# Gathers of an expert's tokens placed behind the last scatter-add of the expert two places ahead, in a mixture-of-experts kernel

## The chip, the cores and the metric

The kernel runs on one core of one Trainium2 chip. Its time is the device time of one execution in microseconds (us), as a median of three runs. Clocks of TensorE are given as the share of full speed that was granted.

## The reference

The program is a chain of three blocks on 2304 tokens of width 512: a linear attention with exponential features, a dense two-layer block with a squared ReLU, and a mixture of 8 experts, each token going to its two best. The change touches the third block alone:

```python
def _moe2_ref(x, w_gate, w_noise, noise, w1, w2):      # x: 2304 x 512, w1: 8 x 512 x 1024, w2: 8 x 1024 x 512
    noisy_logits = x @ w_gate + np.log1p(np.exp(x @ w_noise)) * noise
    top2 = np.argpartition(-noisy_logits, 2, axis=1)[:, :2]
    ...
    for e in range(E):
        for k in range(2):
            mask = top2[:, k] == e
            h = np.maximum(x[mask] @ w1[e], 0.0)
            out[mask] += top2_w[mask, k, None] * (h @ w2[e])
```

## The kernel before

Products are made in 16-bit floating point with every operand split into a high and a low half, so that each product is three matmuls. The dense block leaves its result, rows of 1024 halves, in DRAM (`x2d`). A router writes for each expert a list of 640 slots in five tiles of 128 (`ix`, `ww`: token and weight of each slot).

The experts then go one after the other. For each one the work is:

- **Gather and transpose** (`c_gather`, L583 to L587): GpSimd issues an indirect DMA that fetches the 128 rows of one tile from DRAM into a buffer `g`, of which there are four, and SyncE issues a DMA that transposes it into `xg`. `xg` holds one expert's five tiles and has two buffers: the transposes of expert e+1 need the one that expert e-1 used. Expert 0's first four tiles are gathered earlier, its fifth and all of expert 1's in `c_slots`, during expert 0.
- **First product** (L702): eight tiles of 12 matmuls with 512 columns (`c_main`), then 96 matmuls with 128 columns for the fifth tile of tokens (`c_tail`). The results go to PSUM buffers `c1`, of which there are four. ScalarE (L709) and VectorE (L710) turn each into the halves `hm` of the activation, which frees the buffer.
- **Second product** (L773): five tiles of 24 matmuls. ScalarE scales each result into `y` (L779, three buffers), and GpSimd issues an indirect DMA that adds it to rows of the output (L780). Two scatter-adds can name the same row, so each waits until the one ahead of it has landed.
- **Weights of the next expert** (`c_piece`, L574): eight pieces of 512 KB. For each one ScalarE issues a DMA from DRAM into a staging buffer `stg` (L293, three buffers), makes the high half (L294), and VectorE the low half (L295). These instructions stand in the same queues as L709, L710 and L779, and an engine's queue goes in order: a DMA that ScalarE can't issue yet holds up all that stands behind it.

TensorE's order is the order of the code. For the other engines a scheduler sets the order when the program is built, and it also gives each DMA of SyncE and ScalarE one of eight semaphores (`DMAHW0` to `DMAHW7`, called lanes below), in turn, and each of GpSimd one of `DMASW0` to `DMASW7`. A DMA that gets a lane waits until the lane's last user has landed, unless the program knows that already.

A call of `gathers(e + 1)` stands at the head of expert e (L750 to L751). The scheduler may place its instructions anywhere from there on, or ahead of work that stands earlier in the code, as the buffers allow.

Of the kernel before, what the change touches and what calls it, by code (L numbers as in the profile page):

```python
# [14 lines left out]
ALU = mybir.AluOpType  # L15
# [27 lines left out]
def moe_kernel(tc, qT, kT, v, omT, omD, w_in, w_out, wgn, noise, w1, w2, out):  # L43
    nc = tc.nc
# [523 lines left out]
    def c_weights(e):  # L568
        wp = hC if e % 2 else cP
        a = wp.tile([P, 2, 4, FE], F16, name="w1t", tag="w1t", bufs=1)  # L570
        b = wp.tile([P, 2, 8, DM], F16, name="w2t", tag="w2t", bufs=1)
        W[e] = a, b

    def c_piece(e, j):  # L574
        a, b = W[e]
        if j < 4:
            s = slice(j * 256, (j + 1) * 256)
            split(a[:, 0, :, s], a[:, 1, :, s], w1s[e][:, :, s], [4, 256], SW1)
        else:
            s = slice(j * 2 - 8, j * 2 - 6)  # L580
            split(b[:, 0, s, :], b[:, 1, s, :], w2s[e][:, s, :], [2, 512], SW2)

    def c_gather(xg, t, ix, c, rows=N + P):  # L583
        g = cP.tile([P, 2 * DM], F16, name="g", tag="g", bufs=4)
        nc.gpsimd.indirect_dma_start(out=g, out_offset=None, in_=x2d[0:rows, :],  # L585
                                     in_offset=bass.IndirectOffsetOnAxis(ap=ix[:, c:c + 1], axis=0))
        nc.sync.dma_start_transpose(xg[:, t], g)  # L587
# [3 lines left out]
    def new_xg(e):  # L591
        XG[e] = cP.tile([P, CT, 8, P], F16, name="xg", tag="xg", bufs=2)
# [112 lines left out]
    def c_main(fc, a, xg, e):  # L705
        ps = psC.tile([P, MAIN], F32, name="c1", tag="c1", bufs=4)
        c_mm1(ps, a, e, fc, lambda c: xg[:, 0:4, c, :], lambda c: xg[:, 0:4, 4 + c, :])
        h = hC.tile([P, 2, MAIN], F16, name="hm", tag="hm", bufs=12)
        nc.scalar.activation(h[:, 0], ps, AF.Relu)  # L709
        nc.vector.scalar_tensor_tensor(h[:, 1], ps, 0.0, h[:, 0], ALU.max, ALU.subtract)  # L710
        return h

    def c_tail(g, a, xg, e):
        ps = psC.tile([P, 4, P], F32, name="c1t", tag="c1", bufs=4)
        for i in range(4):
            c_mm1(ps[:, i, :], a, e, 4 * g + i, lambda c: xg[:, 4, c, :], lambda c: xg[:, 4, 4 + c, :])
        h = hC.tile([P, 2, 4, P], F16, name="ht", tag="ht", bufs=3)
        nc.scalar.activation(h[:, 0], ps, AF.Relu)
        nc.vector.scalar_tensor_tensor(h[:, 1], ps, 0.0, h[:, 0], ALU.max, ALU.subtract)
        return h  # L720
# [4 lines left out]
    ix = ww = pm = pg = sp_i = tok = None  # L725

    def c_slots():
        nonlocal ix, ww, pm, pg, sp_i, tok
        next(r5, None)
        ix, ww = slots(0, NCOL, "f")  # L730
        pm = const.tile([P, 1], F32, name="pm")
        nc.vector.tensor_reduce(pm, pall.rearrange("p t k -> p (t k)"), AX.X, ALU.max)
        pg = const.tile([P, 1], F32, name="pg")
        nc.gpsimd.partition_all_reduce(pg, pm, P, bass_isa.ReduceOp.max)
        sp_i = const.tile([P, 1], I32, name="sp_i")
        nc.vector.tensor_copy(sp_i, pg)
        tok = const.tile([P, NT], I32, name="tok")
        nc.gpsimd.iota(tok, [[P, NT]], base=P, channel_multiplier=1)
        c_gather(XG[0], 4, ix, 4)
        gathers(1)  # L740

    def gathers(e):
        new_xg(e)
        for t in range(CT):
            c_gather(XG[e], t, ix, CT * e + t)

    for e in range(NE):
        if e + 1 < NE:
            c_weights(e + 1)
        if 0 < e < NE - 1:  # L750
            gathers(e + 1)  # L751
        a, b = W[e]
        xg = XG[e]
        hm = []
        for fc in range(8):
            hm.append(c_main(fc, a, xg, e))
            if e + 1 < NE:
                c_piece(e + 1, fc)
            if e == 0 and fc in (2, 6):
                next(r5, None)  # L760
        ht = []
        for t in range(CT):
            if t == (3 if e == 0 else 0):
                ht = [c_tail(g, a, xg, e) for g in range(2)]
            ps = psM.tile([P, DM], F32, name="c2", tag="mm", bufs=3)
            n = 0
            for fc in range(8):
                for hl, wl in ((0, 0), (0, 1), (1, 0)):
                    if t < 4:
                        st = hm[fc][:, hl, t * P:(t + 1) * P]  # L770
                    else:
                        st = ht[fc // 4][:, hl, fc % 4, :]
                    nc.tensor.matmul(ps, st, b[:, wl, fc, :], start=n == 0, stop=n == 23)  # L773
                    n += 1
            if e == 0 and t == 0:
                c_slots()
            c = CT * e + t
            y = hC.tile([P, DM], F32, name="y", tag="y", bufs=3)
            nc.scalar.activation(y, ps, AF.Copy, scale=ww[:, c:c + 1])  # L779
            nc.gpsimd.indirect_dma_start(out=out, out_offset=bass.IndirectOffsetOnAxis(ap=ix[:, c:c + 1], axis=0),  # L780
                                         in_=y, in_offset=None, compute_op=ALU.add)
    cctx.close()

    mctx.close()
# [6 lines left out]
    with tc.If(spill > CAP - 1):  # L791
        for e in range(NE):
# [8 lines left out]
            with tc.For_i(0, NT) as t:  # L801
# [19 lines left out]
                for fc in range(8):  # L821
                    for hl, wl in ((0, 0), (0, 1), (1, 0)):
                        nc.tensor.matmul(ps, h[:, hl, fc, :], b[:, wl, fc, :], start=n == 0, stop=n == 23)
                        n += 1
                y = oP.tile([P, DM], F32, name="oy", tag="oy", bufs=1)
                nc.scalar.activation(y, ps, AF.Copy, scale=sc)
                nc.gpsimd.indirect_dma_start(out=out, out_offset=bass.IndirectOffsetOnAxis(ap=oi, axis=0),
                                             in_=y, in_offset=None, compute_op=ALU.add)
# [43 lines left out]
```

## Time and profile before

| | |
|---|---|
| median of three runs | 966.22 us (965.87, 966.22 and 968.92) |
| profiled execution | 967.28 us, of which the span of instructions is 965.4 us |
| mean granted TensorE clock | 0.970 |
| TensorE matmul busy | 914.7 us, 95% of the span |
| VectorE, ScalarE, GpSimd busy | 469.4, 441.7 and 113.0 us |
| mean DMA rate | 131 GB/s |

Times in the profile count from the start of the span. PE is TensorE, DVE VectorE, ACT ScalarE, POOL GpSimd and SP SyncE; a name with q (ACTq, SPq, POOLq) is the engine's queue, which issues DMAs. Idle time of an engine in square brackets names what ended it.

### The profile page before, as it was taken

How to read it: one execution, taken by the hardware profiler on the slowest of the kernel's cores; microseconds unless marked ns; L12 is line 12 of the kernel's file. 1: busy time of each engine (PE TensorE's matmuls, PEld its weight loads, DVE VectorE, ACT ScalarE, POOL GpSimd, SP SyncE). 2: the span in 40 equal slices, each digit the busy share in tenths (PEclk: the TensorE clock that was granted, in tenths of full speed). 3: DMA queues.
4: the chain of work that ended last, by engine and by line, in shares of the span. 5: the costliest groups of instructions: out<-in, count | busy, mean ns of one | idle time of the engine just before them, and what ended most of it. 6: DMA issues, size and time to landing. Idle time of an engine off the chain costs nothing.

```text
span 965.4 us, 15725 instructions
## 1 busy us (share of the span) xinstructions
PE 914.7 (95%) x6254; PEld 501.2 (52%) x6254; DVE 469.4 (49%) x983; ACT 441.7 (46%) x912; POOL 113.0 (12%) x134
## 2 busy tenths in 40 slices
PE   7679799899999999999999997999999999999994
PEld 4546455555655655654654452545454545445451
DVE  4798986772772783584642723333240514230110
ACT  5979975752852862563622423333231423231210
POOL 1000000000000000000001142232222131211111
PEclk8779899999999999999999998999999999999997
DMA  7894787329342114227207499975768595831212
GB/s 240 230 242 136 186 229 170 82 78 296 76 95 66 49 45 99 55 51 183 73 21 171 146 206 212 231 166 117 161 131 175 135 204 121 177 53 24 31 19 40
DMA packets 174723, 126.08 MB, mean 131 GB/s; under 512 B 121744, under 2 KB 147472, under 8 KB 174640
## 3 DMA queue, kind: packets, MB, share of 16 engines
q1 hardware_dynamic: 143072, 74.47, 33.0%
q0 software_dynamic: 9024, 21.08, 12.3%
q10 hardware_dynamic: 22544, 29.43, 10.0%
q8 instruction: 51, 0.84, 0.4%
q14 instruction: 32, 0.26, 0.1%
HBM read 75.15 MB, written 20.45 MB: 99 GB/s over the span
## 4 chain that ended last, share of the span: by engine, by line
PE 71%; ACT 6%; DVE 5%; DMA 5%; issue 2%; POOL 0%; POOLq 0%; DVEq 0%; ACTq 0%
PE s L356 19%; PE c L773 18%; PE c L702 16%; PE s L339 10%; PE c1t L702 4%; ACT ef L175 2%; DMA xg<-g 2%; PE pj L160 2%; DMA out_dram<-y,ix_f 2%; DMA stg<-in_w_dram 1%; DVE r L347 1%; DVE h L348 1%; ACT r L343 1%; ACT eq L179 1%; DVE nm L168 1%
## 5 line engine op out<-in xcount | busy, mean ns | idle before, releaser
L339 PE MATMUL s<-xT,wi 128*128 128x384 f16 x1152 | 198.2, 330 | 3.8 <-ACT r L343 3.7
L356 PE MATMUL s<-wo,h 128*128 128x512 f16 x864 | 192.8, 381 | 3.3 <-ACT r L343 3.3
L702 PE MATMUL c<-xg,w1t 128*128 128x512 f16 x768 | 171.0, 384 | 6.7 <-DVE hm L710 6.6
L702 PEld LDWEIGHTS <-w1t 128*128 128x128 f16 x1536 | 119.2, 98 | 102.0 <-issue 12.1
L773 PE MATMUL c<-w2t,hm 128*128 128x512 f16 x768 | 167.4, 379 | 0.0
L339 PEld LDWEIGHTS <-wi 128*128 128x128 f16 x1152 | 110.8, 99 | 78.6 <-issue 8.2
L356 PEld LDWEIGHTS <-h 128*128 128x128 f16 x864 | 83.5, 98 | 102.1 <-issue 5.7
L773 PEld LDWEIGHTS <-hm 128*128 128x128 f16 x768 | 74.8, 98 | 88.5
L779 ACT ACTIVATE y<-c,ww_f 128x512 f32<-128x512 f32 x40 | 27.5, 687 | 156.1 <-PE c L773 100.8
L295 DVE SCALAR_TENSOR_TENSOR w2t<-stg,w2t 128x1024 f16<-128x1024 f32 x32 | 38.1, 1222 | 124.1 <-ACT w2t L294 124.1
L175 ACT ACTIVATE ef<-pj,nm 128x128 f32<-128x128 f32 x248 | 74.1, 383 | 42.2 <-DVE nm L168 42.1
L780 POOL DMA_INDIRECT out_dram<-y,ix_f x40 | 62.8, 1571 | 170.9 <-ACT y L779 77.2
L710 DVE SCALAR_TENSOR_TENSOR hm<-c,hm 128x512 f16<-128x512 f32 x64 | 43.2, 687 | 78.5 <-ACT hm L709 78.4
L709 ACT ACTIVATE hm<-c 128x512 f16<-128x512 f32 x64 | 37.2, 593 | 66.8 <-PE c L702 60.2
L160 PE MATMUL pj<-om,raw 64*128 64x128 f32 x576 | 51.1, 304 | 13.6 <-ACT ef L175 10.5
L347 DVE TENSOR_TENSOR r<-r 128x384 f32<-128x384 f32 x96 | 53.2, 554 | 16.3 <-ACT r L343 14.4
L343 ACT ACTIVATE r<-s 128x384 f32<-128x384 f32 x96 | 47.3, 494 | 23.2 <-PE s L339 21.3
L348 DVE TENSOR_TENSOR h<-r,h 128x384 f16<-128x384 f32 x96 | 53.4, 556 | 7.6 <-ACT h L345 2.7
L160 PEld LDWEIGHTS pj<-om,raw 64*128 64x128 f32 x576 | 41.7, 202 | 28.5 <-ACT ef L175 12.6
L295 DVE SCALAR_TENSOR_TENSOR w1t<-stg,w1t 128x1024 f16<-128x1024 f32 x32 | 37.8, 1223 | 35.8 <-ACT w1t L294 35.8
L585 POOL DMA_INDIRECT g<-x2d,ix_f x36 | 38.8, 1079 | 135.5 <-DMA xg<-g 127.6
L168 DVE TENSOR_REDUCE nm<-pj 128x4 f32<-128x512 f32 x72 | 47.6, 683 | 9.6 <-PE pj L160 9.6
(158 smaller groups left out, 873.6 us busy)
## 6 DMA issues: line engine op xcount, KB each, us to landing
stg<-in_w_dram ACTq DMA_DIRECT2D x56, 512.0 KB
stg<-in_w_in_dram SPq DMA_DIRECT2D x16, 512.0 KB
stg<-in_w_out_dram SPq DMA_DIRECT2D x16, 512.0 KB
out_dram<-zero SPq DMA_DIRECT2D x19, 256.0 KB
raw<-in_kT_dram SPq DMA_DIRECT2D x9, 512.0 KB
vr<-in_v_dram SPq DMA_DIRECT2D x18, 256.0 KB
raw<-in_qT_dram SPq DMA_DIRECT2D x9, 512.0 KB
x2d<-x SPq DMA_DIRECT2D x18, 256.0 KB
```

Of the source, the lines that this page charges most:

```text
L160: nc.tensor.matmul(pj[g][:, j, :], raw[s, j, :], om[s, :], start=True, stop=True)
L168: nc.vector.tensor_reduce(nm, pj, AX.X, ALU.max, negate=True)
L175: nc.scalar.activation(ef[:, i, :], pj[:, i, :], AF.Exp, bias=nm[:, i:i + 1])
L295: nc.vector.scalar_tensor_tensor(dst_l, stg, scale, dst_h, ALU.mult, ALU.subtract)
L339: nc.tensor.matmul(ps, wi[:, wl, c, fc * P:(fc + 1) * P], x[:, :, xl + c, :], start=n == 0, stop=n == 11)
L343: nc.scalar.activation(r, ps, AF.Relu, scale=SH / (SX * SWI))
L347: nc.vector.tensor_tensor(r2, r, r, ALU.mult)
L348: nc.vector.tensor_tensor(h[:, 1], r2, h[:, 0], ALU.subtract)
L356: nc.tensor.matmul(ps, hs[fc][:, hl, j * P:(j + 1) * P], wo[:, wl, fc, :], start=fc == 0 and k == 0, stop=fc == 15 and k == 2)
L702: nc.tensor.matmul(ps, a[:, wl, c, fc * P:(fc + 1) * P], mv(c), start=n == 0, stop=n == 11)
L773: nc.tensor.matmul(ps, st, b[:, wl, fc, :], start=n == 0, stop=n == 23)
L780: nc.gpsimd.indirect_dma_start(out=out, out_offset=bass.IndirectOffsetOnAxis(ap=ix[:, c:c + 1], axis=0), in_=y, in_offset=None, compute_op ...
```

## The change

The gathers of experts 2 to 7 are told to be issued behind an instruction: the last scatter-add of the expert two places ahead of them. `tc.issue_after` adds no wait on a semaphore, it only fixes the order in GpSimd's queue. Two lines of code move by one or two, so L780 of before is L781 after.

```diff
--- before.py
+++ after.py
@@ -748,7 +748,8 @@
         if e + 1 < NE:
             c_weights(e + 1)
         if 0 < e < NE - 1:
-            gathers(e + 1)
+            with tc.issue_after(added.ins):
+                gathers(e + 1)
         a, b = W[e]
         xg = XG[e]
         hm = []
@@ -777,8 +778,9 @@
             c = CT * e + t
             y = hC.tile([P, DM], F32, name="y", tag="y", bufs=3)
             nc.scalar.activation(y, ps, AF.Copy, scale=ww[:, c:c + 1])
-            nc.gpsimd.indirect_dma_start(out=out, out_offset=bass.IndirectOffsetOnAxis(ap=ix[:, c:c + 1], axis=0),
-                                         in_=y, in_offset=None, compute_op=ALU.add)
+            added = nc.gpsimd.indirect_dma_start(out=out,
+                                                 out_offset=bass.IndirectOffsetOnAxis(ap=ix[:, c:c + 1], axis=0),
+                                                 in_=y, in_offset=None, compute_op=ALU.add)
     cctx.close()
```

GpSimd's queue before, from the second scatter-add of expert 0 to the gathers behind expert 1's scatter-adds (`g` is a gather, `out_dram` a scatter-add; the three gathers at the head are expert 1's last and expert 2's first two):

```order
L780 DMA out_dram<-y,ix_f 2432x512
L585 DMA g<-x2d,ix_f 128x1024 x3
L780 DMA out_dram<-y,ix_f 2432x512
L585 DMA g<-x2d,ix_f 128x1024 x6
L780 DMA out_dram<-y,ix_f 2432x512
L585 DMA g<-x2d,ix_f 128x1024
L780 DMA out_dram<-y,ix_f 2432x512
L585 DMA g<-x2d,ix_f 128x1024 x4
L780 DMA out_dram<-y,ix_f 2432x512
L585 DMA g<-x2d,ix_f 128x1024
L780 DMA out_dram<-y,ix_f 2432x512 x4
L585 DMA g<-x2d,ix_f 128x1024 x4
```

The same queue after, from the same scatter-add on; the one gather ahead of the three scatter-adds is expert 1's last:

```order
L781 DMA out_dram<-y,ix_f 2432x512
L585 DMA g<-x2d,ix_f 128x1024
L781 DMA out_dram<-y,ix_f 2432x512 x3
L585 DMA g<-x2d,ix_f 128x1024 x5
L781 DMA out_dram<-y,ix_f 2432x512 x5
L585 DMA g<-x2d,ix_f 128x1024 x5
L781 DMA out_dram<-y,ix_f 2432x512 x5
```

Before, gathers of up to two experts ahead stand among an expert's scatter-adds; after, five scatter-adds of one expert and five gathers of the expert two places behind it take turns, to the end.

SyncE's transposes keep their order but get other lanes. Before, from the transpose of expert 0's last tile on (then expert 1's five, then expert 2's first three); the last `DMAHW` that a row names is the lane that it takes (one ahead of it guards the buffer), and where none is named its lane was known to be free:

```order
L587 DMA_TRANSPOSE xg<-g 128x8x128 [waits DMAHW0_49,DMASW6_49]
L587 DMA_TRANSPOSE xg<-g 128x8x128 [waits DMAHW1_49,DMASW7_49]
L587 DMA_TRANSPOSE xg<-g 128x8x128 [waits DMAHW2_49,DMASW0_49]
L587 DMA_TRANSPOSE xg<-g 128x8x128 [waits DMAHW3_49,DMASW1_49]
L587 DMA_TRANSPOSE xg<-g 128x8x128 [waits DMAHW4_49,DMASW3_49]
L587 DMA_TRANSPOSE xg<-g 128x8x128 [waits DMAHW5_49,DMASW5_49]
L587 DMA_TRANSPOSE xg<-g 128x8x128 [waits DMAHW0_49,DMAHW6_49,DMASW6_49,PE_49]
L587 DMA_TRANSPOSE xg<-g 128x8x128 [waits DMAHW7_49,DMASW7_49]
L587 DMA_TRANSPOSE xg<-g 128x8x128 [waits DMASW1_49]
```

The first six rows are the same after; the seventh, expert 2's first tile, takes lane 6 before and lane 3 after. ScalarE's queue before, at the end of expert 0 and the start of expert 1 (the loads of `stg` are pieces of expert 2's weights):

```order
L293 DMA stg<-in_w_dram 128x4x256 [waits DMAHW2_49,DVE_49]
L293 DMA stg<-in_w_dram 128x2x512 [waits DMAHW3_49,DVE_49]
L779 ACTIVATE y<-c_6872,ww_f 128x512 [waits DMASW2_49,PE_49]
L294 ACTIVATE w1t<-stg 128x4x256 [waits DMAHW2_49]
L293 DMA stg<-in_w_dram 128x2x512 [waits DMAHW5_49,DVE_49]
L293 DMA stg<-in_w_dram 128x2x512 [waits DMAHW6_49,DVE_49]
L779 ACTIVATE y<-c_6900,ww_f 128x512 [waits DMASW4_49,PE_49]
L294 ACTIVATE w2t<-stg 128x1024 [waits DMAHW3_49]
L294 ACTIVATE w2t<-stg 128x1024 [waits DMAHW5_49]
L709 ACTIVATE hm<-c_6946 128x512 [waits PE_49]
L294 ACTIVATE w2t<-stg 128x1024 [waits DMAHW6_49]
L293 DMA stg<-in_w_dram 128x2x512 [waits DMAHW7_49,DVE_49]
```

The same twelve rows after:

```order
L293 DMA stg<-in_w_dram 128x4x256 [waits DVE_49]
L293 DMA stg<-in_w_dram 128x2x512 [waits DVE_49]
L780 ACTIVATE y<-c_6872,ww_f 128x512 [waits DMASW2_49,PE_49]
L294 ACTIVATE w1t<-stg 128x4x256 [waits DMAHW6_49]
L293 DMA stg<-in_w_dram 128x2x512 [waits DMAHW0_49,DVE_49]
L293 DMA stg<-in_w_dram 128x2x512 [waits DMAHW1_49,DVE_49]
L780 ACTIVATE y<-c_6900,ww_f 128x512 [waits DMASW4_49,PE_49]
L294 ACTIVATE w2t<-stg 128x1024 [waits DMAHW7_49]
L294 ACTIVATE w2t<-stg 128x1024 [waits DMAHW0_49]
L709 ACTIVATE hm<-c_6946 128x512 [waits PE_49]
L294 ACTIVATE w2t<-stg 128x1024 [waits DMAHW1_49]
L293 DMA stg<-in_w_dram 128x2x512 [waits DMAHW2_49,DVE_49]
```

The instructions and their order are the same. The two loads in the fifth and sixth row wait for lanes 0 and 1 in place of lanes 5 and 6. The orders of TensorE and VectorE are the same too.

## Rows read from the trace of the kernel before

**Rows 1.** The page's first part: busy us, share of the span, instructions.

```profile
PE 914.7 (95%) x6254; PEld 501.2 (52%) x6254; DVE 469.4 (49%) x983; ACT 441.7 (46%) x912; POOL 113.0 (12%) x134
```

**Rows 2.** Busy time by stage: from:to, length, each engine's busy us, clock, DMA share.

```profile
580.00:600.00 20.00, 13.36 (x54) 5.48 (x53) 4.79 (x5) 5.32 (x7) 5.31 (x6) 0.90 1.14 218
...
613.20:639.10 25.90, 25.90 (x122) 11.72 (x120) 5.41 (x5) 7.24 (x9) 8.23 (x8) 1.00 0.88 207
639.10:659.80 20.70, 20.70 (x100) 9.45 (x98) 9.38 (x11) 8.54 (x12) 4.46 (x3) 1.00 0.62 141
```

**Rows 3.** Timeline of TensorE, expert 1: start, us, instructions, idle time before them.

```profile
576.79 10.52 PE L702 MATMUL c<-xg,w1t 128*128 128x512 f16 x48
591.42 4.20 PE L702 MATMUL c<-xg,w1t 128*128 128x512 f16 x12 [4.10 <-DVE hm L710]
598.16 9.68 PE L702 MATMUL c<-xg,w1t 128*128 128x512 f16 x36 [2.54 <-DVE hm L710]
607.68 5.52 PE L702 MATMUL c1t<-xg,w1t 128*128 128x128 f16 x96
```

**Rows 4.** The chain that ended last, in order of time: start, us, what.

```profile
572.81 13.35 DMA xg<-g
...
586.24 8.93 DMA stg<-in_w_dram
...
639.11 20.72 PE c L702 x96
659.83 5.36 PE c1t L702 x96
```

**Rows 5.** Timeline of ScalarE and its queue, end of expert 0 and expert 1.

```profile
569.47 1.53 ACTq L293 DMA_DIRECT2D stg<-in_w_dram  x2
...
577.55 1.06 ACT L294 ACTIVATE w1t<-stg 128x1024 f16<-128x1024 f32 x1 [5.04 <-DMA stg<-in_w_dram]
584.08 2.56 ACTq L293 DMA_DIRECT2D stg<-in_w_dram  x2
586.74 0.69 ACT L779 ACTIVATE y<-c,ww_f 128x512 f32<-128x512 f32 x1 [8.13 <-DMA xg<-g]
...
595.25 1.01 ACTq L293 DMA_DIRECT2D stg<-in_w_dram  x2
...
599.29 1.06 ACT L294 ACTIVATE w2t<-stg 128x1024 f16<-128x1024 f32 x1 [2.55 <-DMA stg<-in_w_dram]
```

**Rows 6.** Timeline of VectorE, the conversion behind the one at 577.55.

```profile
578.64 1.23 DVE L295 SCALAR_TENSOR_TENSOR w1t<-stg,w1t 128x1024 f16<-128x1024 f32 x1 [6.91 <-ACT w1t L294]
```

**Rows 7.** Busy time in short stretches of expert 1, columns as in rows 2.

```profile
591.40:598.20 6.80, 4.24 (x13) 1.50 (x13) 1.83 (x2) 1.54 (x2) 0.97 (x2) 0.75 1.05 219
598.20:613.20 15.00, 15.00 (x133) 9.30 (x133) 5.70 (x8) 4.91 (x8) 5.11 (x4) 0.89 0.88 212
```

**Rows 8.** Timeline of ScalarE and its queue in experts 2 and 3.

```profile
642.11 0.37 ACTq L293 DMA_DIRECT2D stg<-in_w_dram  x1
...
646.40 1.06 ACT L294 ACTIVATE w2t<-stg 128x1024 f16<-128x1024 f32 x1 [1.48 <-DMA stg<-in_w_dram]
...
720.03 1.51 ACTq L293 DMA_DIRECT2D stg<-in_w_dram  x2
...
726.70 1.06 ACT L294 ACTIVATE w1t<-stg 128x1024 f16<-128x1024 f32 x1 [3.63 <-DMA stg<-in_w_dram]
```

**Rows 9.** Timeline of GpSimd: gathers (L585) and scatter-adds (L780).

```profile
567.57 0.95 POOL L585 DMA_INDIRECT g<-x2d,ix_f  x1 [0.30 <-issue]
...
571.60 1.62 POOL L780 DMA_INDIRECT out_dram<-y,ix_f  x1 [1.31 <-DMA out_dram<-y,ix_f]
...
599.43 1.62 POOL L780 DMA_INDIRECT out_dram<-y,ix_f  x1 [0.31 <-issue]
604.77 0.99 POOL L585 DMA_INDIRECT g<-x2d,ix_f  x1 [3.73 <-DMA xg<-g]
...
644.49 1.55 POOL L780 DMA_INDIRECT out_dram<-y,ix_f  x1 [4.03 <-DMA out_dram<-y,ix_f]
```

## The prediction

> **What bounds the kernel now.** I read the page first: TensorE is busy for 95% of the span [rows 1]. So only a stretch in which TensorE waits, or runs slowly, can give time back. The busy time by stage shows where that is: between 580 and 600 us TensorE works 13.36 of 20 us at a granted clock of 0.90, while in the two stages behind it is busy for all 25.90 and 20.70 us at full clock [rows 2]. The stretch at 580 to 600 is the first product of expert 1. TensorE's timeline there shows four tiles without a pause, 4.10 us of waiting, one tile, 2.54 us of waiting, then the rest, each time for VectorE's `hm` (L710), which frees a PSUM buffer [rows 3]. The product runs from 576.79 to 607.68 + 5.52 = 613.20, 36.41 us. In expert 2 the same work takes 20.72 + 5.36 = 26.08 us [rows 4]. So 10.33 us are lost in one place, and this is all that the change can win from TensorE.
>
> The loss is 4.10 + 2.54 = 6.64 us of waiting, and some 3.35 us of slow clock: 6.8 us at 0.75 and 15 us at 0.89 [rows 7] are 1.70 + 1.65. The clock has two levels, 1.2 and 2.4 GHz; it fell after TensorE had waited, so the slow part goes with the waits.
>
> Why `hm` is late stands in the chain: a transpose of gathered rows that takes 13.35 us (issued at 572.81), then a weight load, 8.93 us, that ScalarE issues when it has landed [rows 4]. ScalarE's timeline is the mechanism. It issues the weight loads of expert 2 in its own queue. After the conversion at 577.55 the next two issues stand at 584.08 and, 13.35 us after the transpose, at 586.24; `y` of expert 0's last tile, done by TensorE at 576.79, comes only at 586.74, "DMA xg<-g" 8.13 us [rows 3, 5]. Everything behind the issues, `hm` too, waits with them. The order rows say why: these two loads take semaphore lanes 5 and 6, whose last users are the transpose of expert 1's last tile and the first transpose of expert 2.
>
> **The change, step by step.** It adds no instruction and removes none, and TensorE, VectorE, ScalarE and SyncE keep their order. Two things move.
>
> First, the gathers. Nine gathers (five of expert 2, four of expert 3) now leave the queue between 567.57 and 604.77, ahead of or between the scatter-adds; the fourth scatter-add of expert 0 goes out only at 599.43, straight from a gather (0.31 us, "issue") [rows 9]. After the change both last scatter-adds of expert 0 go first. A scatter-add waits for the one ahead of it; the undisturbed period is 1.55 + 4.03 = 5.58 us [rows 9]. The third goes out at 571.60 [rows 9], so the fifth goes at about 571.60 + 11.2 = 582.8, and the five gathers of expert 2 from 584.6 on. GpSimd's waits cost nothing by themselves: expert 2's rows are wanted by TensorE at 639.11 now and about 629 then, over 40 us later.
>
> Second, the lanes. The same two loads take lanes 0 and 1, whose last users are the transposes of expert 0's last and expert 1's first tile, four transposes and more ahead of those that they wait for now. So they wait for their staging buffers alone.
>
> Now the new path. Let L1, L2, L3 be the times that three loads take, each issued when the one before it has been used. The first goes out at 569.47 as now; its conversion on VectorE ends 578.64 + 1.23 − 577.55 = 2.32 us after landing, which frees the buffer for the second [rows 5, 6]; the third goes 0.08 us after the second has landed (595.17 to 595.25); and from a landing to the TensorE work that it holds up it is 598.16 − 595.17 = 2.99 us [rows 4, 5]. So TensorE may go on at 569.47 + 2.32 + 0.08 + 2.99 + L1 + L2 + L3 = 574.86 + sum. TensorE needs this for its seventh tile, as four PSUM buffers stand ahead and the third tile's `hm` is behind the third load: 576.79 + 6 × 20.72/8 = 592.33. It waits only if the sum is over 17.5 us. Today it is 8.08 + 8.93 + 4.04 = 21.05 [rows 4, 5], and the lanes cost another 586.24 − 579.87 = 6.4 us on top.
>
> What a load takes then no row shows, so I bound it. Beside no transpose it takes 646.40 − 642.11 = 4.29 us; beside four transposes and gathers, in the slowest of five such places, 726.70 − 720.03 = 6.67 us [rows 8]. The sum is between 12.9 and 20.0. In the new order expert 1's last transposes are beside the first load, hardly anything beside the second, and the new gathers start about when the third ends. I take 5.5 each, midway: 16.5, ready at 591.4, 0.9 us early. At 20.0 it is ready at 594.9, 2.5 us late. The Trainium skill (DMA: Bandwidth & Descriptors, "Anatomy of one DMA") fits a DMA issued by GpSimd as 2.0 us and its bytes at 436 GB/s. Carried over to a load of 512 KB that is an estimate of 3.2 us each and a sum of 9.6, so no wait; the trace's 4.29 to 8.93 us does not agree with it.
>
> I forecast that 9.8 of the 10.33 us come back; 0.5 is kept for the thin margin. The profiled execution took 967.28 us, of which 965.4 are span, and lies 1.06 above the median of 966.22. So 957.5 for a run like the profiled one, a span of 955.6, and **956.4 us** for the median.
>
> What else the moved gathers touch: in experts 2 to 6 they and their transposes go from the second product of the expert ahead (DMA share 0.88) to the first product of the expert itself (0.62) [rows 2]. There one load per expert stands ahead of an `hm`: issued 642.11 − 639.11 = 3.00 us into the product, needed 15.54 us in, less 2.99: it may take 9.55 us. With 6.67 it is 2.9 us early, so this costs nothing. The rule that speaks against the change is in the Trainium skill (DMA: Bandwidth & Descriptors, "Issuing engines are not separate DMA queues"): transfers of all queues run on the same 16 DMA engines and interleave. By it the moved transfers slow that load; the trace agrees so far as 6.67 stands against 4.29, which does not reach 9.55. The end of the kernel keeps its chain of scatter-adds, since no gather stands among them before or after.
>
> **Rivals.**
> A, partial: loads stay as slow as today (21.05) because expert 1's own transposes and the loads, not the moved gathers, fill the DMA engines. Then TensorE waits until 595.9, 3.6 us, and one slow clock stretch stays (half of 3.35). The gain is 10.33 − 5.3 = 5.0: 961.2 us. For it: the first load is issued beside expert 1's transposes in either case. Against: five other transposes and nine gathers leave that stretch.
> B, no change: the wait moves. Expert 2's gathers, now at 584.6 or earlier, and their transposes meet the third load, which then takes the 13.35 us of the slowest transfer in the chain. The sum is 5.5 + 5.5 + 13.35 = 24.4, ready at 599.2, 6.9 us late, as many as the 6.64 of now: 966.2. Against: by the sums above this load goes out at 582.9 and lands near 588.4, as the first gathers do.
> C, slower: in experts 2 to 6 the moved transfers push the load ahead of `hm` over 9.55 us. At 11 us, each of five experts loses 1.45 and a slow clock stretch of about 1.7, 15.7 in all, less the 9.8: 972.1. It decides from about 9.8 us on, where 5 × (0.25 + 1.7) eats the gain. For it: 13.35 has been seen. Against: that was at a DMA share of 1.14 [rows 2], and there are 0.62 to fill up first; with transposes beside it a later load took 6.67.
> That the change does nothing is ruled out by the order rows.
>
> **How the numbers follow.** Forecast (a gain of 8 or more) 0.70, A 0.17, B 0.07, C 0.06. Within 0.3% (2.9 us) is about what a measurement of this kernel can't tell from no change. So faster is forecast and A, 0.87; same 0.07; slower 0.06. The low end is the whole 10.33 and the fastest run's 0.35 below the median: 955.5, say 955.3. The high end takes in A with the lower part of its own scatter: 962.0. That leaves out B, C and few more.
>
> **What would show it.** Right: in the profile after, expert 1's first product takes 26 to 28 us, from 576.8 to about 603; ScalarE's two issues of loads come within about 3 us of the conversion ahead of them; `y` of expert 0's last tile comes before 580; GpSimd shows fives of gathers behind fives of scatter-adds; experts 2 to 7 keep 52.0 us. Wrong: a wait of over 3 us for L710 in expert 1 (A or B, told apart by whether it is the third load alone that is slow), or waits in experts 2 to 6 (C).

## The result, and the profile after

The changed kernel takes **955.45 us** (median of 6 runs, 954.84 to 956.93) against 964.81 us for the kernel before (6 runs, 960.94 to 968.92, the three of the forecast among them): a ratio of **0.9916, 95% interval 0.9889 to 0.9943**. On a second chip it took 956.44 us against 963.74, ratio 0.9922 (0.9890 to 0.9955); a ratio of 0.990 to 0.995 and 954 to 956 us were expected there. The forecast was 956.4 us, range 955.3 to 962.0.

The profiled execution took 955.51 us, its span is 953.6 us, 11.8 less than before. The page's first part answers to [rows 1], and below it stands the row of the first products from its fifth part (busy us, mean ns | idle time before):

```profile
PE 910.5 (95%) x6254; PEld 500.4 (52%) x6254; DVE 469.7 (49%) x983; ACT 442.6 (46%) x912; POOL 117.2 (12%) x134
...
L702 PE MATMUL c<-xg,w1t 128*128 128x512 f16 x768 | 167.3, 379 | 0.0
```

The last number is the idle time of TensorE ahead of all 768 matmuls with 512 columns of the eight first products: none. TensorE's timeline in expert 1 answers to [rows 3]:

```profile
575.50 20.88 PE L702 MATMUL c<-xg,w1t 128*128 128x512 f16 x96
596.22 5.52 PE L702 MATMUL c1t<-xg,w1t 128*128 128x128 f16 x96
```

One piece of 96 matmuls in place of three, and no brackets. The product takes 596.22 + 5.52 − 575.50 = 26.24 us, where it took 36.41: 10.17 back. Of the other 1.6 us, 1.29 lie ahead of this stage (it starts at 575.50, not 576.79). They are not the change's: in eleven more traces of the kernels below (all but the one with six staging buffers) the stage starts anywhere between 573.80 and 577.90. The busy time by stage answers to [rows 2] (from:to, length, each engine's busy us, clock, DMA share, GB/s):

```profile
580.00:600.00 20.00, 20.00 (x144) 11.13 (x143) 8.52 (x12) 6.62 (x11) 7.34 (x7) 1.00 0.99 236
603.00:629.00 26.00, 26.00 (x123) 11.76 (x121) 4.83 (x5) 7.29 (x10) 6.30 (x4) 1.00 0.62 123
```

TensorE is busy for all 20 us at full clock where it had 13.36 us at 0.90, and the DMA share fell from 1.14 to 0.99. The second row is expert 1's second product: 0.62, where it had 0.88. ScalarE's timeline answers to [rows 5]:

```profile
568.17 1.51 ACTq L293 DMA_DIRECT2D stg<-in_w_dram  x2
...
572.90 1.06 ACT L294 ACTIVATE w1t<-stg 128x1024 f16<-128x1024 f32 x1 [1.69 <-DMA stg<-in_w_dram]
572.96 2.66 ACTq L293 DMA_DIRECT2D stg<-in_w_dram  x2
575.72 0.69 ACT L780 ACTIVATE y<-c,ww_f 128x512 f32<-128x512 f32 x1 [1.76 <-PE c L774]
...
579.96 0.37 ACTq L293 DMA_DIRECT2D stg<-in_w_dram  x1
...
584.68 1.06 ACT L294 ACTIVATE w2t<-stg 128x1024 f16<-128x1024 f32 x1 [3.08 <-DMA stg<-in_w_dram]
```

The two issues behind the conversion come at 572.96 and, as the second of the pair ends, at about 575.25 (572.96 + 2.66 less 0.37), when VectorE's conversion has freed the buffer; before, they came at 584.08 and 586.24. `y` of expert 0's last tile comes at 575.72, as soon as TensorE has made it, and not 10 us later. Three loads on the path take 572.9 − 568.17 = 4.7, 579.96 − 575.25 = 4.7 and 584.68 − 579.96 = 4.7 us, where they took 8.08, 8.93 and 4.04. GpSimd's timeline answers to [rows 9]:

```profile
569.55 2.31 POOL L781 DMA_INDIRECT out_dram<-y,ix_f  x1 [3.33 <-ACT w1t L294]
578.13 1.92 POOL L781 DMA_INDIRECT out_dram<-y,ix_f  x1 [6.27 <-ACT w2t L294]
584.12 1.55 POOL L781 DMA_INDIRECT out_dram<-y,ix_f  x1 [4.08 <-DMA stg<-in_w_dram]
585.98 1.91 POOL L585 DMA_INDIRECT g<-x2d,ix_f  x1 [0.30 <-issue]
...
607.93 1.62 POOL L781 DMA_INDIRECT out_dram<-y,ix_f  x1 [9.05 <-ACT y L780]
...
632.12 2.20 POOL L781 DMA_INDIRECT out_dram<-y,ix_f  x1 [4.16 <-ACT hm L709]
634.62 1.02 POOL L585 DMA_INDIRECT g<-x2d,ix_f  x1 [0.30 <-issue]
```

Five scatter-adds, then five gathers, and so on. Expert 1's first scatter-add goes out at 607.93, straight behind its `y`.

### The profile page after: what moved, and what is told of

Read it like the earlier page. It is cut to its first block, busy times and chain, and to the rows that moved or that the text cites. A ratio compares the mean times of both kernels' runs of the same rounds, so it can differ in the third digit from the quotient of the medians.

```text
span 953.6 us, 15721 instructions
## 1 busy us (share of the span) xinstructions
PE 910.5 (95%) x6254; PEld 500.4 (52%) x6254; DVE 469.7 (49%) x983; ACT 442.6 (46%) x912; POOL 117.2 (12%) x134
## 4 chain that ended last, share of the span: by engine, by line
PE 76%; ACT 6%; DVE 5%; issue 1%; DMA 1%; POOL 0%; POOLq 0%; DVEq 0%; ACTq 0%
PE c L774 21%; PE s L356 19%; PE c L702 17%; PE s L339 10%; PE c1t L702 4%; ACT ef L175 2%; PE pj L160 2%; DVE r L347 1%; DVE h L348 1%; DMA out_dram<-y,ix_f 1%; ACT r L343 1%; ACT eq L179 1%; DVE nm L168 1%; ACT h L345 1%; ACT L452 0%
## 5 line engine op out<-in xcount | busy, mean ns | idle before, releaser
L702 PE MATMUL c<-xg,w1t 128*128 128x512 f16 x768 | 167.3, 379 | 0.0
L780 ACT ACTIVATE y<-c,ww_f 128x512 f32<-128x512 f32 x40 | 27.5, 688 | 152.2 <-PE c L774 140.8
L781 POOL DMA_INDIRECT out_dram<-y,ix_f x40 | 66.6, 1664 | 235.5 <-ACT y L780 102.4
L710 DVE SCALAR_TENSOR_TENSOR hm<-c,hm 128x512 f16<-128x512 f32 x64 | 43.9, 688 | 92.9 <-ACT hm L709 92.7
L345 ACT ACTIVATE h<-r 128x384 f16<-128x384 f32 x96 | 51.1, 533 | 2.0
```

Source lines behind the costliest of these rows:

```text
L345: nc.scalar.activation(h[:, 0], r, AF.Square)
L702: nc.tensor.matmul(ps, a[:, wl, c, fc * P:(fc + 1) * P], mv(c), start=n == 0, stop=n == 11)
L781: added = nc.gpsimd.indirect_dma_start(out=out, out_offset=bass.IndirectOffsetOnAxis(ap=ix[:, c:c + 1], axis=0), in_=y, in_offset=None, co ...
```

## The experiments

Ratios are to the kernel before on the same chip, with 95% intervals; lines behind L740 shift by a few in some kernels. The kernel before took 961.0, 963.74, 963.05 and 963.95 us on the chips of the four groups of runs.

**Only the gathers of expert 2 tied.**

```diff
-            with tc.issue_after(added.ins):
+            with (tc.issue_after(added.ins) if e == 1 else ExitStack()):
                 gathers(e + 1)
```

> Only the gathers of expert 2 are tied; those of experts 3 to 7 are free as in the kernel before. My theory, that all that the change gives comes from expert 1's first product, expects the whole gain: 955.5 us within 1, ratio 0.990 to 0.993, expert 1's first product at 26 to 27 us without a wait for L710, its two loads on the same lanes (0 and 1) as with all ties. Rival, that the ties of the later experts have a part in it: 957.5 to 963, with waits or a slower clock in experts 2 to 6. GpSimd now issues up to thirteen gathers in a row behind expert 0's last scatter-add, so by the rival that piled-up transfers slow the loads the third load takes over 8 us and expert 1 shows a wait again.

Measured: 958.3 us, ratio 0.9979 (0.9948 to 1.0010). My theory falls: the gain is a quarter of the 0.8% that all ties give in the two comparisons above, and two thirds at most by the interval's low end. On this same chip the changed kernel with its lanes put back (a later experiment), which ties all gathers, took 954.66 us. Expert 1's first product is whole (26.24 us, no wait), but TensorE's timeline shows two waits later, in experts 2 and 4:

```profile
643.35 12.95 PE L702 MATMUL c<-xg,w1t 128*128 128x512 f16 x48 [4.30 <-DVE hm L710]
751.34 10.52 PE L702 MATMUL c<-xg,w1t 128*128 128x512 f16 x48 [1.45 <-DVE hm L710]
```

GpSimd's timeline of the same run, and ScalarE's below it, show how they come about. The traced execution took 964.65 us, 6.35 more than the median; five of the twelve took 955.6 to 957.4, so it is not shown that these waits come in each:

```profile
622.24 0.94 POOL L585 DMA_INDIRECT g<-x2d,ix_f  x1 [2.61 <-DMA xg<-g]
626.02 0.94 POOL L585 DMA_INDIRECT g<-x2d,ix_f  x1 [2.84 <-DMA xg<-g]
627.27 1.62 POOL L781 DMA_INDIRECT out_dram<-y,ix_f  x1 [0.30 <-issue]
```

```profile
632.15 0.69 ACT L780 ACTIVATE y<-c,ww_f 128x512 f32<-128x512 f32 x1 [13.10 <-DMA out_dram<-y,ix_f]
637.53 0.69 ACT L780 ACTIVATE y<-c,ww_f 128x512 f32<-128x512 f32 x1 [4.69 <-DMA out_dram<-y,ix_f]
638.12 2.94 ACT L294 ACTIVATE w2t<-stg 128x1024 f16<-128x1024 f32 x3
```

Thirteen gathers stand in a row, and from the fifth on most of them wait for transposes, which free the four buffers `g`. Expert 1's first scatter-add stands behind them and goes out at 627.27, some 19 us later than with all ties. The three `y` buffers are full by then: ScalarE stands at the fourth `y` for 13.10 us, with the weight conversions and `hm` of expert 2 behind it. So the ties of the later experts do have a worth, in such executions: they keep scatter-adds from standing behind gathers that can't go.

**The same with six `y` buffers.**

```diff
-            y = hC.tile([P, DM], F32, name="y", tag="y", bufs=3)
+            y = hC.tile([P, DM], F32, name="y", tag="y", bufs=6)
```

> The kernel that ties only the gathers of expert 2, with six buffers for y in place of three; orders and lanes are the same as with three. With three it took 958.3 us median, and its trace shows expert 1's first scatter-add at 627.27 us behind nine further gathers that each wait for a transpose, then y, hm and TensorE late in expert 2 (4.30 us) and expert 4 (1.45 us). Theory: untied gathers of the later experts cost because they hold up scatter-adds, and these hold the three y buffers and so ScalarE's queue. Then six buffers give it all back: 954.5 to 956 us, GpSimd's order and its late scatter-adds as before, no wait for L710 in experts 2 to 6. Rival, that the later gathers cost by their transfers beside the weight loads: no gain, 957.5 to 959 us, with the waits where they were.

Measured: 957.22 us, ratio 0.9921 (0.9890 to 0.9952), that of all ties on the same chip (0.9922); in us it lies between the two ranges that I had set. Its trace has no wait for L710 at all. Expert 1's first scatter-add is still late, behind the last of thirteen gathers:

```profile
619.32 0.94 POOL L585 DMA_INDIRECT g<-x2d,ix_f  x1 [2.52 <-DMA xg<-g]
620.57 1.62 POOL L781 DMA_INDIRECT out_dram<-y,ix_f  x1 [0.30 <-issue]
```

That bears out the second mechanism: the gathers and the scatter-adds are as late, and with room for `y` TensorE waits for none of it. None of the seven executions passed 959.85 us, where five of twelve did with three buffers, on another chip.

**The kernel before with six `y` buffers**, the same edit.

> The kernel before with six buffers for y in place of three; all orders and lanes are the same. In the trace of before, hm in expert 1 is late because issues of loads wait for transposes, and experts 2 to 6, untied as they are, lose nothing. Theory, that before's loss is expert 1's alone: no gain, ratio 0.998 to 1.002, waits for L710 in expert 1 as before. Rival, that scatter-adds held up by gathers, which cost so much where only expert 2 was tied, are also a part of what before loses: ratio 0.992 to 0.997.

Measured: 962.06 us, ratio 0.9982 (0.9957 to 1.0007): no gain that can be told from none, though the interval leaves room for the upper part of the rival's range. In its trace TensorE waits 4.05 + 0.82 + 1.54 us in expert 1's first product, and nowhere later.

**Only the gathers of experts 3 to 7 tied.**

```diff
-            with tc.issue_after(added.ins):
+            with (tc.issue_after(added.ins) if e > 1 else ExitStack()):
                 gathers(e + 1)
```

> The reverse: the gathers of experts 3 to 7 are tied, those of expert 2 are free, so the five of expert 2 and their transposes stay beside expert 1's last transposes and the loads keep lanes 5 and 6; only the four gathers of expert 3 leave the stretch, and these went out from 588 us on. My theory expects little: 963 to 966 us, the two issues of loads at about 584 and 586 us, and a transpose of over 10 us ahead of them. Rival, that the number of transfers in the stretch is all that counts and not which of them the issues wait for: 958 to 961, since four of the nine moved gathers are gone. Rival, that the later ties give something: the same 958 to 961, but with the waits of expert 1 as they were.

Measured: 960.89 us, ratio 0.9993 (0.9968 to 1.0018): without the first tie the others are worth nothing that can be measured, as the theory has it. In us the run lies in the range of the rivals, 958 to 961, but the ranges were set by the times of the first comparison (964.81 us before), and the kernel before took 961.0 here. ScalarE's queue, and TensorE:

```profile
578.71 1.90 ACTq L293 DMA_DIRECT2D stg<-in_w_dram  x2
580.71 0.69 ACT L780 ACTIVATE y<-c,ww_f 128x512 f32<-128x512 f32 x1 [5.26 <-DMA xg<-g]
```

```profile
587.75 2.75 PE L702 MATMUL c<-xg,w1t 128*128 128x512 f16 x12 [1.17 <-DVE hm L710]
592.55 4.44 PE L702 MATMUL c<-xg,w1t 128*128 128x512 f16 x12 [2.05 <-DVE hm L710]
597.39 5.34 PE L702 MATMUL c<-xg,w1t 128*128 128x512 f16 x24 [0.41 <-DVE hm L710]
```

The issues are held as before, though less (578.71 and about 580.2, not the 584 and 586 expected), and hm is late.

**The lanes of before put back into the changed kernel**, by small DMAs that take a lane each:

```diff
-        gathers(1)
+        last = gathers(1)
+        with tc.issue_after(last.ins):
+            for k in range(5):
+                nc.sync.dma_start(const.tile([1, 8], F32, name=f"lane{k}"), w1s[0][0:1, 0, 0:8])
```

(`c_gather` and `gathers` return the transpose for it, here and below.)

> The changed kernel with five DMAs of 32 bytes each put behind the transpose of expert 1's last tile in SyncE's queue. They shift the lanes so that the first of the two loads waits for the transpose of expert 1's last tile (lane 5), as in the kernel before, and the second for the first of the small DMAs behind it; GpSimd's order is that of the changed kernel. My theory says that a lane costs only as much as its last user is late, and that it was late because of expert 2's transfers: in the changed kernel the transpose of expert 1's last tile lands at 576.5 us, so the load goes out at 576.6 in place of 572.96, the next at about 576.7 in place of 575.25, and TensorE, which had some 3 us of margin, waits for nothing: 955.5 us within 1. Rival, that the assignment of lanes is the cause by itself: over 959 us with a wait for L710 in expert 1.

Measured: 954.66 us, ratio 0.9938 (0.9915 to 0.9961), no wait. ScalarE's queue and TensorE's first product:

```profile
575.50 0.90 ACTq L293 DMA_DIRECT2D stg<-in_w_dram  x2
```

```profile
573.80 20.88 PE L702 MATMUL c<-xg,w1t 128*128 128x512 f16 x96
```

The issues are held until the transpose has landed, about 3 us past the point at which the buffer was free, and nothing is lost. Which lane a load gets is not the cause by itself.

**Three further transposes beside the loads, early lanes.** Early lanes are those whose last users landed long before the loads want them, late lanes those of transposes that may still be under way.

```diff
+        d = hC.tile([P, 2 * DM], F16, name="d")
+        nc.vector.memset(d, 0.0)
+        with tc.issue_after(last.ins):
+            for k in range(3):
+                nc.sync.dma_start_transpose(hC.tile([P, 8, P], F16, name=f"dT{k}"), d)
```

> The changed kernel with three more transposes of a constant tile (128x1024 halves) in SyncE's queue, right behind the transpose of expert 1's last tile: the transfers of expert 2's first three transposes come back, while the lanes of the two loads stay with early users (the transposes of expert 1's third and fourth tile). Theory, that slow transposes cost only where an issue waits for one of them: the loads get slower, to 5.5 to 7 us each, a sum of 16.5 to 20 against the 17.5 that TensorE bears, so 955 to 958 us with a wait of at most 2 us in expert 1. Rival, that the transfers beside the loads are the cause by themselves: loads of 8 to 9 us as in the kernel before, a wait of 3.6 us and a stretch of slow clock, 959.5 us or more.

Measured: 957.97 us, ratio 0.9931 (0.9904 to 0.9959). The loads got slower, as expected: the second on the path goes out at about 577.1 (574.83 + 2.66 less 0.38) and is used at 585.21, 8.1 us:

```profile
574.83 2.66 ACTq L293 DMA_DIRECT2D stg<-in_w_dram  x2
...
585.21 1.06 ACT L294 ACTIVATE w2t<-stg 128x1024 f16<-128x1024 f32 x1 [1.34 <-DMA stg<-in_w_dram]
...
589.75 1.06 ACT L294 ACTIVATE w2t<-stg 128x1024 f16<-128x1024 f32 x1 [3.00 <-DMA stg<-in_w_dram]
```

TensorE does not wait for `hm`. Slower loads alone are borne too, here just so (the path is 20.0 us long, and it bears 19.9: see the next section).

**Five further transposes, late lanes** (the same with `range(5)`).

> The same with five further transposes, which also shifts the lanes: the two loads wait for the transpose of expert 1's last tile and for the first further transpose, and the load behind them for the second, as in the kernel before they wait for expert 1's last and expert 2's first and second. GpSimd's order is that of the changed kernel. Theory, that slow transposes and issues that wait for them make the loss together: 959 to 964 us, the issues of loads several us behind the conversion ahead of them, and one or two waits for L710 in expert 1. Rival, that the gathers among the scatter-adds (GpSimd's order) are needed for the loss: 955 to 956.5 us, as without the transposes. Rival, that transfers alone do it: the same as with three further transposes.

Measured: 961.14 us, ratio 0.9962 (0.9935 to 0.9988): about half of the gain is gone again (956.44 us without the transposes on the same chip), while GpSimd's order is that of the changed kernel. The rival by which GpSimd's order is needed for the loss falls. The trace taken with it was far off the median (978.21 us), so a second one was taken:

> The changed kernel with five further transposes once more: its first trace was of an execution of 978 us, far over its median of 961.14, so this is a look at a usual one. Theory: 958 to 965 us, the issues of the two loads held by the transpose of expert 1's last tile and the first further one, 6 to 9 us behind where three further transposes leave them, and 2 to 5 us of waits for L710 in expert 1.

That execution took 964.68 us, with one wait of 5.76 us in expert 1:

```profile
595.51 10.20 PE L702 MATMUL c<-xg,w1t 128*128 128x512 f16 x36 [5.76 <-DVE hm L710]
```

```profile
578.82 0.37 ACTq L293 DMA_DIRECT2D stg<-in_w_dram  x1
...
592.54 1.06 ACT L294 ACTIVATE w2t<-stg 128x1024 f16<-128x1024 f32 x1 [7.10 <-DMA stg<-in_w_dram]
```

The place is right, the split is not: the issue at 578.82 came little over 1 us late by held issues, since the conversion ahead of it stood behind one, and it is the load that took 592.54 − 578.82 = 13.7 us beside the transposes. That left open what the held issues cost, so the last run has the traffic of three transposes and the lanes of five.

**Three further transposes, late lanes.**

```diff
             for k in range(3):
                 nc.sync.dma_start_transpose(hC.tile([P, 8, P], F16, name=f"dT{k}"), d)
+            for k in range(2):
+                nc.sync.dma_start(hC.tile([1, 8], F32, name=f"lane{k}"), w1s[0][0:1, 0, 0:8])
```

> Three further transposes, as in the kernel that lost next to nothing by them (ratio 0.9931), and behind them two DMAs of 32 bytes each, which shift the lanes to those of the kernel with five: the loads wait for the transpose of expert 1's last tile and for the first two further ones. What was left open is whether the five transposes cost by their transfers (in the last look one load took 13.7 us beside them) or by the issues that wait for them. By the trace with three, the first further transpose lands at 582.26 us, where the second load of the path went out at 577.12; held until then it lands at about 590, the third at about 595, and TensorE goes on some 3 to 5 us late. Theory, that issues held by slow transposes are a part of the cause of their own: 959.5 to 963 us, ratio 0.996 to 1.0, a wait for L710 in expert 1. Rival, that the transfers beside the loads are all of it: as with three, 956 to 958.5 us, ratio 0.992 to 0.995, no wait.

Measured: 956.63 us, ratio 0.9933 (0.9906 to 0.9960), no wait: what the rival gives. My 3 to 5 us did not come.

```profile
567.03 2.75 ACTq L293 DMA_DIRECT2D stg<-in_w_dram  x2
...
576.71 1.19 ACTq L293 DMA_DIRECT2D stg<-in_w_dram  x2
578.00 0.69 ACT L788 ACTIVATE y<-c,ww_f 128x512 f32<-128x512 f32 x1 [5.34 <-DMA dT<-d]
...
583.40 0.90 ACTq L293 DMA_DIRECT2D stg<-in_w_dram  x2
...
587.06 1.06 ACT L294 ACTIVATE w2t<-stg 128x1024 f16<-128x1024 f32 x1 [2.17 <-DMA stg<-in_w_dram]
```

The second issue of the pair is held to about 577.5 by a further transpose ("DMA dT<-d"), 3.6 us past the 571.60 + 2.32 at which the buffer is free. But in this execution, the fastest of the ten (954.92 us), the loads were short, some 14 us in sum, and the third is used at 587.06, 20.0 us behind the first issue: about what TensorE bears (next section). What such issues cost beside slower loads stays open. I had taken the transposes' landing times from one execution of another kernel.

**Six staging buffers in the kernel before.**

```diff
-        stg = work.tile([P] + shape, F32, name="stg", tag="stg", bufs=3)
+        stg = (hC or work).tile([P] + shape, F32, name="stg", tag="stg", bufs=6 if hC else 3)
```

> The kernel before, with six staging buffers for the weight loads in the expert stage in place of three; the orders of GpSimd and SyncE are those of before. The loads that were slow (8.08, 8.93 and 4.04 us) go out earlier and are off the path, but ScalarE's queue still holds issues that wait for transposes: two at lanes 0 and 1 until about 584 and 586 us, and further ones among hm for expert 2's second to fourth transpose, about 587, 595 and 597.5 us. My theory, that hm is late because issues wait for these transposes, expects only a part back: TensorE goes on with its fifth tile at about 590.5 and its eighth at about 598.8, some 4 us of waits and 1.5 of slow clock, 960 to 962.5 us. Rival, that the slow loads alone were the path: 955 to 957 us. Rival, that more loads in flight slow the transposes further: 966 or more.

Measured: 964.32 us, ratio 1.0041 (1.0010 to 1.0073), a little slower; the rival of more loads in flight is nearest, but not as I had it. TensorE's timeline:

```profile
564.69 7.03 PE L702 MATMUL c1t<-xg,w1t 128*128 128x128 f16 x96 [4.52 <-DMA xg<-g]
...
581.92 21.17 PE L702 MATMUL c<-xg,w1t 128*128 128x512 f16 x96
...
647.81 10.52 PE L702 MATMUL c<-xg,w1t 128*128 128x512 f16 x48 [3.10 <-DVE hm L710]
```

In expert 1's first product nothing waits any more, although ScalarE's issues are still held: by its timeline three issues from 577.00 on take 10.51 us. The loads that count had landed before. But the stage also starts some 5 us later, so that this trace doesn't show that held issues alone are borne. Three early loads go out from 551.25 on, beside the gather of expert 0's last tile (551.79), and TensorE waits for that tile 4.52 us. In expert 2 it waits 3.10 us, after ScalarE has stood at a `y` for 11.94 us until a scatter-add landed.

**The kernel before, a second trace.**

> The kernel before once more, for a second look at its trace. Its times on the two chips above spread from 956 to 972 us, those of the changed kernel from 954 to 960. Theory: what varies is how late expert 1's last and expert 2's first transposes are, so the time goes with the waits for L710 in expert 1's first product: some 956 us without a wait there, 961 with 3 us of it, 966 with 6 to 7. Rival: waits in experts 2 to 6, of which the first trace showed none.

That execution took 962.81 us, with 4.08 us of waits in expert 1 and 1.53 in expert 2:

```profile
585.34 2.75 PE L702 MATMUL c<-xg,w1t 128*128 128x512 f16 x12 [0.87 <-DVE hm L710]
591.30 10.73 PE L702 MATMUL c<-xg,w1t 128*128 128x512 f16 x36 [3.21 <-DVE hm L710]
645.18 10.82 PE L702 MATMUL c<-xg,w1t 128*128 128x512 f16 x48 [1.53 <-DVE hm L710]
```

```profile
633.72 0.69 ACT L779 ACTIVATE y<-c,ww_f 128x512 f32<-128x512 f32 x1 [10.06 <-DMA out_dram<-y,ix_f]
```

The theory has the larger part, the rival the smaller: ScalarE waits 10.06 us there for a scatter-add, as in the first experiment. So the kernel before had this second weakness as well; in the execution on which I predicted, the longest such wait of ScalarE behind expert 1 was 8.6 us, and TensorE did not wait.

## Why the prediction was right, step by step

**The loss in expert 1.** Right: 10.17 of 10.33 us came back there, and what is left is not to be told from the usual 26.1 us.

**The path: buffer, load, load, load, hm.** This is the step that the runs bear out best. I had TensorE ready at the first issue plus 5.39 us plus three loads, late once the loads pass 17.5 us. In other words: from the first issue to the use of the third load may pass 17.5 + 2.32 + 0.08 = 19.9 us, held issues counted in. Each trace gives both sides, the length from ScalarE's rows and the loss as the length of expert 1's first product less 26.24 (in each the product starts 7.3 us behind the first issue):

| kernel | first issue, third load used | length | less 19.9 | loss |
|---|---|---|---|---|
| before, first trace | 569.47, 599.29 | 29.82 | 9.9 | 10.17 |
| before, six `y` buffers | 568.04, 596.46 | 28.42 | 8.5 | 8.52 |
| five transposes, second trace | 569.31, 597.06 | 27.75 | 7.9 | 8.19 |
| before, second trace | 566.61, 592.67 | 26.06 | 6.2 | 7.21 |
| experts 3 to 7 tied | 568.72, 594.42 | 25.70 | 5.8 | 5.80 |
| three transposes, late lanes | 567.03, 587.06 | 20.03 | 0.1 | 0.13 |
| three transposes, early lanes | 569.73, 589.75 | 20.02 | 0.1 | 0.11 |
| lanes put back | 566.47, 584.60 | 18.13 | none | 0.00 |
| after, second trace | 570.58, 588.05 | 17.47 | none | 0.00 |
| after, first trace | 568.17, 584.68 | 16.51 | none | 0.00 |
| expert 2 alone tied | 569.21, 585.69 | 16.48 | none | 0.00 |

The loss, waits and slow clock together, is the length less 19.9 within 1.1 us over eleven traces. Three are left out: the trace with six staging buffers, where the stage starts late; the one with expert 2 alone tied and six `y` buffers, where the product has 1.0 us of gaps that the profile puts down to issue and not to `hm`; and the first trace with five transposes, of an execution of 978.21 us, where the length is 38.93, 19.0 over, and the loss 21.51.

The table also says what the change took away: 6.4 us of held issues and 21.05 − 14.0 = 7 us of slower loads. Neither is shown to be the cause by itself: by these sums, which no run tried one by one in the kernel before, with either gone the length would have been 22.8 or 23.4 (29.82 less 7.0 or 6.4), still some 3 us too long. The other three traces of the table in which expert 2's gathers are free put more on the loads. These take 20.1, 19.7 and 19.8 us in sum, and issues are held for 3.6, 6.3 and 3.5 us (before's second trace, six `y` buffers, experts 3 to 7 tied). Without held issues all three would still be over 19.9 by 2 us and more; with loads of 14.0 the first and the third would come to 19.9.

**The lanes.** Right as a mechanism, too strong as I put it: "the lanes cost another 6.4 us" is true only on top of slow loads. With late lanes beside no further transposes, and beside three, they cost nothing in the traced executions.

**The loads' size.** I took 5.5 us each, sum 16.5; they took 4.7 each, 14.0 together, near the lower bound of 12.9. So the 0.5 us that I kept back for a thin margin wasn't needed: 3.4 us were to spare (2.4 in the second trace after). The Trainium skill's fit (DMA: Bandwidth & Descriptors, "Anatomy of one DMA") gave an estimate of 3.2 us a load; the trace's 4.7 does not agree. The Trainium skill's rule that DMAs of all issuing engines run on the same 16 DMA engines and interleave (DMA: Bandwidth & Descriptors, "Issuing engines are not separate DMA queues") fits the traces: the load that took 4.7 us took 8.1 and 5.8 beside three further transposes and 13.7 beside five.

**GpSimd.** The fifth scatter-add came at 584.12 (said: 582.8), the gathers at 585.98 (584.6): the fourth went out 8.6 us behind the third, not 5.6. That the third landed late, among loads and transposes, is likely but not shown.

**Experts 2 to 6.** Nothing was lost, and for a stronger reason than mine. I bore a load of 6.67 us ahead of `hm` beside the moved gathers; in the trace it goes out at 630.65 and is used at 634.79, 4.1 us, and the gathers start at 634.62, when it is over. What I missed is that the ties of these experts gain something: without them scatter-adds stand behind gathers that wait, which ends in waits of 4.30 + 1.45 us in the first experiment's trace and 1.53 in the second trace of before.

**The sum.** 957.5 was forecast for the profiled run and 955.51 came: 0.4 us from the margin not needed, 1.29 from ahead of the stage, the rest from behind it. The median lies 0.15 us above the low end of the range, and that it came within 1 us of the forecast is in part luck. I took a gain of 9.8 off the 966.22 of three runs; the medians give 9.36 here and 7.30 on the second chip. The trace that I read lost more in expert 1 (10.17 us) than the other three of the table with expert 2's gathers free (8.52, 7.21 and 5.80). **The rivals.** A needed loads of 21.05 us in sum (14.0 came), B a third load that meets the gathers (it was used at 584.68, the first gather went out at 585.98: clear by 1.3 us), C a load of over 9.55 us ahead of `hm` (4.1).

## What to carry to other kernels

Before a load, a product or a lane is blamed, add up the whole path from one buffer to the engine that waits, with what that engine can bear: delays that are each borne alone can be a loss together. In a queue that goes in order, look at what stands behind the instruction that can't go: gathers that wait for a buffer hold up scatter-adds, these hold `y`, and the matmuls are late some 16 us on, in another expert; a fixed order and a few more buffers each cured it here. More buffers for one transfer can cost elsewhere, by meeting a transfer that was on time.

## What the runs showed of the hardware

One load of 512 KB on this path took from 3.7 us (587.06 − 583.40, the third with three transposes and late lanes) to 13.7 us (the second with five) in the traces of the table. The kernel before spread from 956.0 to 972.7 us over all chips. The changed one took 954.8 to 960.2, and its two traces stay clear of the line at 19.9 us by 2.4 and 3.4; that the loads make the spread of the kernel before is likely, but only two of its executions were traced. TensorE's mean granted clock between 580 and 600 us was 1.00 in the traces without a wait for `hm` there, and 0.90, 0.83 and 0.91 in before, in the second trace with five transposes and in the run with experts 3 to 7 tied; these are means of the levels 2.4 and 1.2 GHz. So a wait costs more than itself: 8.19 us in all for one of 5.76.
